# Issuing the last 64 rows of a projection weight before its first 384 rows, at the head of a transfer-bound decode kernel

## The chip, the cores and the metric

The kernel runs on one core of one Trainium2 chip. The metric is device time in microseconds (us) of one execution; a kernel's time is the median of its runs. "The trace" is one profiled execution. In a trace, PE is the matmul engine, DVE the vector engine, ACT the scalar engine, POOL the general one, and SP the engine whose sequencer issues nearly all transfers here; "SPq" is that sequencer. PEld stands for PE's weight loads. A transfer is moved in packets (here of up to 64 KB) by 16 transfer engines. It is issued when SP hands it over, and it has landed when its last bytes have arrived. L438 is line 438 of the kernel.

## The reference, cut to what matters

One token attends to a cache of 65536 positions (16 query heads, 8 key/value heads, head size 256). A small gated block is added. All data are bfloat16.

```
q      = x @ wq                           # x: [1,448]   wq: [448,4096]
scores = einsum(q, k_cache) / 16          # k_cache: [8, 65536, 256]
p      = softmax(scores)
a      = einsum(p, v_cache) @ wo          # v_cache: [8, 65536, 256], wo: [4096,448]
h      = relu(x @ W_gate) * (x @ W_up)    # [448,1792] each
b      = h @ W_down
g      = sigmoid(sum(x * gate_w))
out    = g * a + (1 - g) * b
```

The two caches are 512 MiB. Everything else is some 12 MB.

## The kernel before: the parts that matter here

A planner collects operations with a key, sorts each engine's operations by key, and adds the semaphore waits. A transfer's key is thus its place in SP's order. A cache tile of 8 MB is 128 partitions of 64 KB; three such buffers form a ring. The projection weights at the start borrow the third buffer.

wq has 448 = 3 x 128 + 64 rows. The first 384 are loaded as three rows per partition (24 KB contiguous, "the long rows"), the last 64 as half a row per partition (4 KB, "the short rows"). The matmuls of q need both.

```
for kind, i, t in issue:
    if kind == "wq":
        l_["wq"]  = dma("sp", t,        "wq",  ... dma_start(wq3, A_wq[0:NR3, :].rearrange("(p k) n -> p (k n)", k=R3)))
        l_["wqh"] = dma("sp", t + 0.01, "wqh", ... dma_start(wqh, A_wq[NR3:D, :].rearrange("r (t n) -> (r t) n", t=2)))
        l_["q"]   = mop("pe", tq, f_q, [l_["wq"], l_["wqh"], q0])
        ...                                # q is spread into xm, which the scores need
    elif kind == "gu":                     # gate and up weights: long and short rows each
        ...
    elif kind == "wd":                     # lands over wq, so it waits for q
        a3 = dma("sp", t, "wd", ..., [l_["q"]])
    elif kind == "k":
        kd = dma("sp", t, "r%d" % sl, ... dma_start(ring[sl][:], k_src(n)), free(("k", n)))
```

SP's order at the start is: wq long, wq short, first k tile, gate and up weights, then (after q is computed) wd, then k tiles and v tiles as buffers come free.

## Time and profile before

The time before is 1277.79 us (median of 3 runs, 1277.51 to 1278.08).

| what | value | view |
|---|---|---|
| bytes moved, mean rate | 549.22 MB, 430 GB/s | transfers of the page |
| share of the span in which PE, DVE, ACT are busy | 33%, 50%, 5% | busy times of the page |
| long rows of wq: issue, then time to landing | 0.72 us, 10.5 us | timeline, table of issues |
| short rows of wq: issue, then time to landing | 1.19 us, 11.3 us | timeline, table of issues |
| first q matmul, end of q | 12.53 us, 21.46 us | timeline |
| first DVE work on the k tile | 31.82 us | timeline |

From the page of the kernel before: busy times, then the span in 40 slices with the busy tenths of the transfer engines and the rate in each slice, then packet counts.

```profile
PE 426.9 (33%) x4568; PEld 167.3 (13%) x4568; DVE 633.4 (50%) x421; ACT 63.3 (5%) x124; POOL 4.1 (0%) x21
...
DMA  9999999999999999999999999999999999999998
GB/s 398 443 433 430 435 429 438 435 431 429 435 433 440 428 429 435 433 440 429 431 435 431 438 431 433 435 431 432 438 431 431 435 431 438 433 429 435 415 444 348
DMA packets 12948, 549.22 MB, mean 430 GB/s; under 512 B 1283, under 2 KB 3590, under 8 KB 3974
```

The transfers are 90% or more busy in every slice but the last, at an even rate. No compute engine comes near that. The time is the bytes divided by the rate, plus a short head and a short tail.

Table of transfer issues of the kernel before: destination and source, engine, count, KB each, us from issue to landing.

```profile
ring<-in_A_wq_dram SPq DMA_DIRECT2D x1, 3072.0 KB, 10.5
...
ring<-in_A_wq_dram SPq DMA_DIRECT2D x1, 512.0 KB, 11.3
ring<-in_A_k_cache_dram SPq DMA_DIRECT2D x32, 51.3
ring<-in_A_v_cache_dram SPq DMA_DIRECT2D x31, 33.5
```

A tile takes about 19.4 us to move, but 33 to 51 us (medians) from issue to landing: the queue behind the 16 engines is never empty in the steady state.

Timeline of the kernel before, the lines that matter of its first 35 us: start, length, engine, line, operation, and in brackets how long the engine was idle before it and what ended that.

```profile
0.72 0.40 SPq L437 DMA_DIRECT2D ring<-in_A_wq_dram  x1
1.19 0.41 SPq L438 DMA_DIRECT2D ring<-in_A_wq_dram  x1
1.65 0.43 SPq L483 DMA_DIRECT2D ring<-in_A_k_cache_dram  x1
...
12.53 8.93 PE L341 MATMUL QN<-ring,P_sb 128*128 128x512 bf16 x32 [3.12 <-DMA ring<-in_A_wq_dram]
...
21.49 0.33 SPq L471 DMA_DIRECT2D ring<-in_B_W_down_dram  x1
...
31.82 4.50 DVE L367 STREAM_TRANSPOSE ring<-ring 128x2048 uint32<-128x2048 uint32 x2 [7.50 <-DMA ring<-in_A_k_cache_dram]
```

SP issues the next transfer (wd, L471) as soon as q ends at 21.49 us. At that time the queue still holds the k tile and the gate and up weights, so q is early.

### The profile page before, as it was taken

Reading aid. Unit: us, or ns where it says so; the run is one execution under the profiler, and the core shown is the slowest. Engines: PE = TensorE matmul, PEld = TensorE weight load, DVE = VectorE, ACT = ScalarE, POOL = GpSimd, SP = SyncE. Lnnn points to the kernel's source line nnn. Section 1 sums busy time; section 2 is a strip of 40 time slices with the busy share of each in tenths; the row PEclk is TensorE's granted clock in tenths of the full one; section 3 lists DMA queues with packets and bytes.
Section 4 is the critical chain, followed back from the end, with each engine's and each line's share of the span. In section 5 each row is a group of like instructions: output and inputs, shape, how many; then the busy total and the mean of one; then the engine's idle time right before and its main releaser. Section 6 shows DMA issues by size and latency. Waiting matters only on the chain. (4 is left out here: it accounts for less than half of the span.)

```text
span 1276.2 us, 10216 instructions
## 1 busy us (share of the span) xinstructions
PE 426.9 (33%) x4568; PEld 167.3 (13%) x4568; DVE 633.4 (50%) x421; ACT 63.3 (5%) x124; POOL 4.1 (0%) x21
## 2 busy tenths in 40 slices
PE   3633322334223431224331343321333313233255
PEld 1501110111001210002110111100111101011021
DVE  2698633465433655434555444555434655335600
ACT  0000000010000100001000010000100001000000
POOL 1000000000000000000000000000000000000000
PEclk9656666656666565666656666656666656666565
DMA  9999999999999999999999999999999999999998
GB/s 398 443 433 430 435 429 438 435 431 429 435 433 440 428 429 435 433 440 429 431 435 431 438 431 433 435 431 432 438 431 431 435 431 438 433 429 435 415 444 348
DMA packets 12948, 549.22 MB, mean 430 GB/s; under 512 B 1283, under 2 KB 3590, under 8 KB 3974
## 3 DMA queue, kind: packets, MB, share of 16 engines
q1 hardware_dynamic: 12930, 549.03, 99.7%
q8 instruction: 8, 0.13, 0.0%
q14 instruction: 6, 0.05, 0.0%
q10 hardware_dynamic: 4, 0.00, 0.0%
HBM read 549.03 MB, written 0.00 MB: 430 GB/s over the span
## 5 line engine op out<-in xcount | busy, mean ns | idle before, releaser
L367 DVE STREAM_TRANSPOSE ring<-ring 128x2048 uint32<-128x2048 uint32 x256 | 565.4, 2275 | 396.5 <-DMA ring<-in_A_k_cache_dram 396.5
L378 PE MATMUL ST<-ring,xc 128*16 128x512 bf16 x2048 | 223.9, 611 | 745.6 <-PEq L86 745.6
L378 PEld LDWEIGHTS ST<-ring,xc 128*16 128x16 bf16 x2048 | 68.3, 120 | 887.0 <-issue 886.1
L409 PE MATMUL O<-ring,ptp 128*4 128x512 bf16 x2048 | 150.7, 457 | 32.7 <-DMA ring<-in_A_v_cache_dram 18.7
L494 ACT ACTIVATE P_sb<-ST,nmb 128x512 bf16<-128x512 f32 x32 | 45.1, 1410 | 1102.2 <-DVE nmb L492 1102.2
L492 DVE TENSOR_REDUCE nmb<-ST 128x1 f32<-128x512 f32 x32 | 22.0, 689 | 116.8 <-PE ST L378 116.8
L409 PEld LDWEIGHTS O<-ring,ptp 128*4 128x4 bf16 x2048 | 56.4, 99 | 126.6 <-issue 69.3
L419 DVE CAST o_sb<-O 128x512 bf16<-128x512 f32 x8 | 5.5, 691 | 78.6 <-PE O L409 78.6
L513 DVE TENSOR_TENSOR P_sb<-P_sb,hs 128x1024 bf16<-128x1024 bf16 x16 | 18.9, 1221 | 9.4 <-ACT hs L507 9.4
L518 PE MATMUL PT<-identb,P_sb 128*128 128x128 bf16 x128 | 16.2, 307 | 16.8 <-PEq L86 15.8
L459 PE MATMUL M_ps<-xT,ring 128*128 128x1 bf16 x84 | 9.5, 205 | 17.2 <-DMA ring<-in_B_W_up_dram 17.2
L518 PEld LDWEIGHTS PT<-identb,P_sb 128*128 128x128 bf16 x128 | 12.4, 138 | 19.2 <-issue 19.2
L527 ACT COPY ptp<-PT 128x256 bf16<-128x256 bf16 x32 | 10.3, 375 | 23.9 <-PE PT L518 23.9
L341 PE MATMUL QN<-ring,P_sb 128*128 128x512 bf16 x32 | 8.9, 448 | 3.1 <-DMA ring<-in_A_wq_dram 3.1
L459 PEld LDWEIGHTS M_ps<-xT,ring 128*128 128x128 bf16 x84 | 7.2, 152 | 17.8 <-issue 17.4
L494 ACT ACTIVATION_READ_ACCUMULATOR P_sb<-ST,nmb 128x1 f32 x32 | 8.4, 262 | 0.0
L462 PE MATMUL M_ps<-xT,ring 128*64 128x1 bf16 x56 | 7.8, 276 | 0.0
L442 DVE STREAM_TRANSPOSE scr<-P_sb 128x256 uint32<-128x256 uint32 x1 | 0.4, 445 | 12.5 <-ACT P_sb L441 12.5
L503 PE MATMUL M_ps<-identf,hs 128*2 128x128 f32 x8 | 2.5, 308 | 11.1 <-PEq L86 11.1
L539 DVE RECIPROCAL hs<-M_ps 128x2 f32<-128x2 f32 x8 | 1.4, 170 | 8.3 <-PE M_ps L538 8.3
L462 PEld LDWEIGHTS M_ps<-xT,ring 128*64 128x64 bf16 x56 | 5.4, 191 | 0.4
L389 PE MATMUL A_ps<-ring,attnT 128*1 128x224 bf16 x64 | 4.6, 306 | 0.7 <-DMA ring<-in_A_wo_dram 0.6
(74 smaller groups left out, 65.7 us busy)
## 6 DMA issues: line engine op xcount, KB each, us to landing
ring<-in_A_v_cache_dram SPq DMA_DIRECT2D x1, 4096.0 KB, 23.6
ring<-in_A_wq_dram SPq DMA_DIRECT2D x1, 3072.0 KB, 10.5
ring<-in_A_wo_dram SPq DMA_DIRECT2D x1, 2240.0 KB, 38.3
ring<-in_A_v_cache_dram SPq DMA_DIRECT2D x1, 2048.0 KB, 28.2
ring<-in_B_W_down_dram SPq DMA_DIRECT2D x1, 1568.0 KB, 21.7
ring<-in_B_W_gate_dram SPq DMA_DIRECT2D x1, 1344.0 KB, 32.9
ring<-in_B_W_up_dram SPq DMA_DIRECT2D x1, 1344.0 KB, 35.5
ring<-in_A_v_cache_dram SPq DMA_DIRECT2D x1, 1024.0 KB, 30.2
```

The lines of the kernel that those rows point to most:

```text
L341: ins = e.matmul(QN_ps, xw3[:, k_, 31 - h:159 - h], rhs, start=(h == 0 and kt == 0), stop=(h == H - 1 and kt == R3))
L367: return lambda e: e.transpose(v, v)
L378: ins = e.matmul(bank[32 * w:32 * w + 16, :], xc[:, x0:x0 + 16], ktv[sl][:, u0:u0 + 16, c, :, r_], start=(b == 0 and c == 0 and r_ == 0), ...
L409: ins = e.matmul(OP[32 * g:32 * g + 4, :], ptp[:, col:col + 13:4], ring[sl][:, k * 512:(k + 1) * 512], start=(a == 0 and k < 4), stop=(a = ...
L419: o1 = op("dv", tn, lambda e: e.tensor_copy(o_sb[:], OP[:]), [pv[n], last.get(("otr", h - 1))])
L459: e.matmul(GU_ps[:, c:c + 1], wf3[which][:, kt * F + ft:(kt + 1) * F:FT], xT[:, kt:kt + 1], start=(kt == 0), stop=False, skip_group_check= ...
L462: ins = e.matmul(GU_ps[64 * half:64 * half + 64, c:c + 1], wfh[which][:, ft:F // 2:FT], xT[:, R3 + half:R3 + half + 1], start=False, stop= ...
L492: smax[n] = op("dv", tk + 22, lambda e, n=n, NM=NM, t_=t_: e.tensor_reduce(NM[:, t_:t_ + 1], ST[n % 2][:], AX.X, ALU.max, negate=True), [q ...
L494: aexp[n] = op("ac", tk + 23, lambda e, n=n, t_=t_, NM=NM, RS=RS: e.activation(P_sb[:, t_:2048:4], ST[n % 2][:], ACTF.Exp, bias=NM[:, t_:t ...
L513: rsc = op("dv", tt, lambda e, X=X, pb=pb: e.tensor_tensor(pb, pb, X[:, 12:16].unsqueeze(1).to_broadcast([128, 256, 4]), ALU.mult), [h7, a ...
L518: ins = e.transpose(PT[rd][:, s * 128:(s + 1) * 128], P_sb[:, (rd * 8 + s) * 128:(rd * 8 + s + 1) * 128], identb[:, :])
L527: ins = e.copy(dst, src)
```

## The change

The intent: the short rows are small and were the last thing that q waited for, so they go first.

```diff
-                l_["wqh"] = dma("sp", t + 0.01, "wqh", lambda e: e.dma_start(wqh, A_wq[NR3:D, :].rearrange("r (t n) -> (r t) n", t=2)))
+                l_["wqh"] = dma("sp", t - 0.01, "wqh", lambda e: e.dma_start(wqh, A_wq[NR3:D, :].rearrange("r (t n) -> (r t) n", t=2)))
```

No bytes, packets or instructions change; two issues on SP swap places.

## The prediction

> **What bounds the kernel now.** The transfers. The page of the profile gives 549.22 MB in a span of 1276.2 us, a mean of 430 GB/s, and the DMA row of its slices is 9 (90% or more busy) in 39 of 40 slices, at 428 to 443 GB/s in all but the first (398) and the last few. The Trainium skill ("DMA: Bandwidth & Descriptors", section "Where 436 GB/s comes from") puts the ceiling of the 16 SBUF ports at 435 GB/s; this trace's slices lie at it. DVE is 50% busy, PE 33%. The chain of waits holds the end of the transfers (32.48 us of wo), then about 3 us of PE and DVE work.
>
> **What the change does.** No bytes, packets or instructions are added or removed. The order of instructions shows one difference on the SP queue: the 512 KB transfer of wq's last 64 rows (128 x 2048, 4 KB per partition) is issued before the 3072 KB one (128 x 12288, 24 KB per partition).
>
> **Costing it.**
> - Issue: the timeline shows the two issues at 0.72 and 1.19 us, 0.40 and 0.41 us long, the k tile's at 1.65. Swapped, k stays at about 1.65.
> - A gap behind the small transfer? At 430 GB/s its 512 KB are an estimated 1.2 us of work, and the next issue follows 0.47 us after it, so the engines should not run dry.
> - The first consumer, the q projection on PE (line 341), waits for both transfers. The table of issues gives 10.5 us to landing for the long one (0.72 + 10.5 = 11.2 us) and 11.3 us for the short (1.19 + 11.3 = 12.5); PE starts at 12.53. After the change the short one should land early (an estimated 3 to 5 us) and the long one at about 12.5, since the same 3.5 MB lie ahead.
> - If q shifts, it has room: it ends at 21.49 us and releases only the issue of wd, while the queue already holds the k tile and the gate and up weights, which land until about 39.5 us. That is 18 us of slack. Later tiles are issued with 33 to 51 us to landing, so the queue never empties.
>
> **On the critical path:** essentially nothing. Only the start could move: when the first bytes flow, and the skew of the 16 engines. The one microsecond from 1 to 2 us shows 271 GB/s, so a change of at most some 0.3 us there is thinkable in either direction.
>
> **Predicted time:** 1277.7 us; 8 times in 10 between 1276.0 and 1279.6 us (run to run 0.6 us before). Faster by over 2%: 0.5%; within 2%: 99%; slower by over 2%: 0.5%.
>
> **What would show it right:** the same 549.22 MB, 12948 packets and 430 GB/s; DMA slices all 9; SP issues short, then long, then k at about 1.65 us; the short transfer landing within about 5 us of its issue and the long one taking about 11.5 us; PE's first q matmul at 12.0 to 13.0 us; k's first transpose on DVE at about 31.8 us as before.
> **Wrong:** a first slice well under or over 398 GB/s, a hole in the DMA windows between 1 and 4 us, or a k tile landing a microsecond or more earlier or later.
>
> **What would make it wrong:** small 4 KB packets first starting the engines unevenly, with a skew that lasts to the end; or a cost of the first transfer that depends on its size.

## The result

The changed kernel takes 1277.46 us (median of 6 runs, 1277.28 to 1277.77) against 1277.65 us (median of 6, 1277.39 to 1278.08). The ratio is 0.9998 with a 95% interval of 0.9986 to 1.0011: the same. Ratios here are the mean time of one kernel's fast runs over that of the other's of the same rounds, so not quite the ratio of the medians quoted.

From the page of the changed kernel, the same lines.

```profile
DMA  9999999999999999999999999999999999999998
GB/s 401 448 427 428 436 431 440 433 429 431 436 438 436 428 429 438 436 436 429 429 438 431 438 433 429 433 436 434 436 431 429 436 433 436 433 431 436 405 446 354
DMA packets 12948, 549.22 MB, mean 430 GB/s; under 512 B 1283, under 2 KB 3590, under 8 KB 3974
```

Table of transfer issues of the changed kernel.

```profile
ring<-in_A_wq_dram SPq DMA_DIRECT2D x1, 3072.0 KB, 10.4
...
ring<-in_A_wq_dram SPq DMA_DIRECT2D x1, 512.0 KB, 3.4
```

Timeline of the changed kernel.

```profile
0.73 0.40 SPq L438 DMA_DIRECT2D ring<-in_A_wq_dram  x1
1.19 0.41 SPq L437 DMA_DIRECT2D ring<-in_A_wq_dram  x1
1.65 0.43 SPq L483 DMA_DIRECT2D ring<-in_A_k_cache_dram  x1
...
11.67 8.87 PE L341 MATMUL QN<-ring,P_sb 128*128 128x512 bf16 x32 [3.81 <-DMA ring<-in_A_wq_dram]
...
20.58 0.33 SPq L471 DMA_DIRECT2D ring<-in_B_W_down_dram  x1
...
31.01 4.50 DVE L367 STREAM_TRANSPOSE ring<-ring 128x2048 uint32<-128x2048 uint32 x2 [7.60 <-DMA ring<-in_A_k_cache_dram]
```

The start did change. q begins 0.86 us earlier, wd is issued 0.91 us earlier, and the k tile is usable 0.81 us earlier. The span moved from 1276.2 to 1276.1 us. So two questions are left: where did 0.8 us go, and was it the change's at all?

**Where it went.** The Trainium skill ("DMA: Bandwidth & Descriptors", section "Why a DMA increments its semaphore by 16 and not by 1") says that a transfer runs on up to 16 engines which finish independently, and that only the full count of 16 means that the data have landed. The trace agrees: it has 16 completions for each large transfer, 0.4 to 4 us apart in the six traces of the two kernels. From these records I worked out the first, mean and last completion, in us from the start of the span:

```
                       k tile 0             tile before 868 us       next tile                last transfer of all
                       first mean  last     first  mean   last       first  mean   last       first   mean    last
before                 30.73 31.00 31.80    854.89 855.99 857.59     874.25 875.41 877.25     1272.08 1272.77 1273.92
before, 2nd look       30.73 31.03 31.64    854.91 856.00 857.04     874.26 875.41 877.30     1272.63 1273.06 1274.13
before, 3rd look       30.84 31.47 33.28    854.99 856.42 858.98     874.35 875.83 878.33     1273.42 1274.00 1275.14
after                  30.54 30.73 30.99    854.84 855.77 856.85     874.19 875.18 877.10     1272.25 1272.77 1273.86
after, 2nd look        30.49 30.76 30.98    854.80 855.76 856.88     874.14 875.18 877.20     1272.42 1272.90 1274.06
after, 3rd look        30.43 30.66 30.96    854.73 855.65 856.72     874.08 875.06 876.97     1271.71 1272.48 1273.69
```

A consumer waits for the last of the 16, and the last is what came 0.81 us earlier at the k tile. The mean, which counts the work of all engines, came only 0.27 us earlier. The two leads were lost at different places.

*The lead of the last engine.* While the queue does not run dry, an engine that is late can stay late: in the first two profiles (before and after) the last completion is still 0.74 us apart at 857 us. It need not: in the second look of before the last completion there, 857.04, is only 0.16 us behind the second look of after. Between the first two profiles the lead is then lost in one tile. The latest five of the 16, in nanoseconds after the tile's first:

```
           tile before 868 us              next tile
before     1623 1667 2020 2051 2693        1621 1676 2040 2709 3003
after      1621 1725 1788 1918 2010        1633 1738 1789 2001 2908
```

In both kernels one engine drops by some 0.9 to 1 us in this tile and becomes the last (the records do not name the engines; this is read from the sorted times): in before it was among those at 2020 and 2051 (the old last, 2693, is still there at 2709), in after it was at 1918 or 2010. The last engine of the start is no longer the last engine, and so its lead is worth nothing any more: 877.25 against 877.10 us. Both traces hold an 8 KB instruction packet of 0.33 us at 868.5 and 868.4 us, which may be what this engine was kept by; that is inferred from the time alone, no run takes the packet away.

*The lead of the mean.* It is untouched by this: 0.22 to 0.24 us in the first and second looks, at 857 us and still at 1210 us. Most of it goes in the next tile (0.02 and 0.09 us are left), where the queue nearly runs dry. SP can issue that tile only when PE is done with the scores of the last k tile (releaser PE ST L378 in SP's waits), and these wait for DVE's transposes, which wait for the last of the k tile's 16 completions. Timelines of before and then of after, window 1185 to 1209 us, the lines of this chain:

```profile
1186.91 17.66 DVE L367 STREAM_TRANSPOSE ring<-ring 128x2048 uint32<-128x2048 uint32 x8 [12.18 <-DMA ring<-in_A_k_cache_dram]
1204.77 3.29 PE L378 MATMUL ST<-ring,xc 128*16 128x512 bf16 x32 [5.16 <-PEq L86]
1208.11 0.34 SPq L550 DMA_DIRECT2D ring<-in_A_v_cache_dram  x1
```

```profile
1186.78 17.66 DVE L367 STREAM_TRANSPOSE ring<-ring 128x2048 uint32<-128x2048 uint32 x8 [12.59 <-DMA ring<-in_A_k_cache_dram]
1204.63 3.59 PE L378 MATMUL ST<-ring,xc 128*16 128x512 bf16 x32 [5.15 <-PEq L86]
1208.27 0.34 SPq L550 DMA_DIRECT2D ring<-in_A_v_cache_dram  x1
```

At the issue only one transfer of 2240 KB is left in the queue, and the first engine is done with it about 1 us later (in the third look of before, 0.2 us earlier). From the completions and the packets, in us ("engines idle" is the mean over the 16 engines from 1205 to 1232 us; most other tiles follow each other at 19.35):

```
                    DVE starts     issue of    mean completion           from mean   engines
                    on k tile      next tile   2240 KB      next tile    to mean     idle
before              1186.91        1208.11     1210.36      1230.03      19.67       0.07
before, 2nd look    1186.97        1208.43     1210.34      1230.18      19.84       0.13
before, 3rd look    1188.00        1209.49     1210.72      1231.22      20.50       0.71
after               1186.78        1208.27     1210.13      1230.01      19.88       0.20
after, 2nd look     1186.94        1208.43     1210.12      1230.09      19.97       0.29
after, 3rd look     1186.68        1207.88     1210.00      1229.72      19.72       0.15
```

From here on the transfers follow this issue: over all 14 traces of this document the next tile's mean completion comes 21.7 to 22.1 us after it. In the first pair the changed kernel's k tile was usable 0.13 us earlier, but its last matmuls took 0.30 us longer (3.59 against 3.29), so the issue came 0.16 us later and the engines that were ahead stood idle. At the end the means are equal and the last completions 0.06 us apart. The third look of after had the early issue and kept its 0.3 us. This is read from the traces; no run changes this wait.

### The profile page after: what moved, and what is told of

Its sections match the earlier page's. It is cut to its first block, busy times and chain, and to the rows that moved or that the text cites. A ratio compares the mean times of both kernels' runs of the same rounds, so it can differ in the third digit from the quotient of the medians.

```text
span 1276.1 us, 10216 instructions
## 1 busy us (share of the span) xinstructions
PE 427.3 (33%) x4568; PEld 167.5 (13%) x4568; DVE 633.2 (50%) x421; ACT 63.3 (5%) x124; POOL 4.6 (0%) x21
## 2 busy tenths in 40 slices
DMA packets 12948, 549.22 MB, mean 430 GB/s; under 512 B 1283, under 2 KB 3590, under 8 KB 3974
## 5 line engine op out<-in xcount | busy, mean ns | idle before, releaser
L378 PE MATMUL ST<-ring,xc 128*16 128x512 bf16 x2048 | 222.8, 608 | 745.5 <-PEq L86 745.5
L378 PEld LDWEIGHTS ST<-ring,xc 128*16 128x16 bf16 x2048 | 68.0, 120 | 886.1 <-issue 884.8
L492 DVE TENSOR_REDUCE nmb<-ST 128x1 f32<-128x512 f32 x32 | 22.1, 689 | 116.8 <-PE ST L378 116.8
```

The source lines that it names most:

```text
L378: ins = e.matmul(bank[32 * w:32 * w + 16, :], xc[:, x0:x0 + 16], ktv[sl][:, u0:u0 + 16, c, :, r_], start=(b == 0 and c == 0 and r_ == 0), ...
L492: smax[n] = op("dv", tk + 22, lambda e, n=n, NM=NM, t_=t_: e.tensor_reduce(NM[:, t_:t_ + 1], ST[n % 2][:], AX.X, ALU.max, negate=True), [q ...
```

## The experiments

Theory A: the total of the transfers is the time; q's start has slack; only an empty queue would cost. Rival B: the start of q lies on the critical path, and its gain is kept or should be.

### The changed kernel and the kernel before, again

No edit. First the changed kernel in five rounds:

> The changed kernel once more, in five rounds. Theory A (the transfers' total is the time; the start of q has slack): ratio 0.9999 to 1.0000 of before, at most 0.3 us shorter. Rival B (what q gains at the start is kept to the end): about 0.8 us shorter, ratio 0.9994. In its profile, if the earlier q start belongs to the change and not to one execution: short rows landed about 3.4 us after issue, first q matmul near 11.7 us, k tile's first transpose near 31.0 us.

Measured: 1277.55 us (5 runs, 1277.37 to 1277.64) against 1277.88 us (9 runs, 1277.35 to 1278.06), ratio 0.9998, interval 0.9984 to 1.0011, just outside what theory A was given. First q matmul at 11.63 us, k tile at 31.00 us.

> The kernel before against itself: ratio 1.0000; how far it is off says what a difference of a few tenths of a microsecond is worth. In its profile, if the late q start belongs to the order: first q matmul near 12.5 us, k tile's first transpose near 31.8 us. If it was one execution's: between 11.6 and 12.6 us.

Measured: 1277.59 us (1277.47 to 1277.86) against the same 1277.88 us, ratio 0.9999, interval 0.9985 to 1.0013. First q matmul at 12.37 us, k tile at 31.67 us.

> One more look at the changed kernel, for the spread of the start from execution to execution: first q matmul 11.5 to 11.9 us if the earlier start belongs to the change.

Measured: first q matmul at 11.66 us, k tile at 30.98 us. (The state of a single run is unknown; single runs serve here for positions in the trace, not for times.)

> One more look at the kernel before: first q matmul 12.3 to 12.7 us if the late start belongs to the order; nearer 11.7 us if it was one execution's.

Measured: first q matmul at 12.37 us; the run was 1278.65 us, and being single its state is unknown.

What follows: the earlier q start belongs to the change (11.63 to 11.67 us in three traces, 12.37 to 12.53 us in three of before). Against the same 9 runs the changed kernel was 0.33 us shorter and the kernel before itself 0.29 us shorter. So a few tenths of a microsecond can't be told apart here, but the 0.8 us of rival B is not there. A weaker rival is left open: over all runs the medians are 1277.70 us for before (36 runs, single ones included) and 1277.46 for after (12), so some 0.2 us of the mean's lead may on average be kept.

The odd run before_look is instructive, with the caution that it is one run. Some of its engines were held up between 12 and 33 us: the last completion of the k tile came at 33.28 us, 1.49 us later than in the first trace of before. The last completion of the last transfer came 1.22 us later, at 1275.14, and the span was 1.2 us longer, 1277.4. The table above shows how: at 1210 us the mean was only some 0.4 us behind that of the first trace of before, but the last engine's lag delayed the last k tile by 1.09 us and the issue behind it by 1.38, the other engines stood idle, and the mean was 1.19 us behind at 1231. A lag of the last engine costs the span where a wait for it lets the queue run dry.

### Moving q by much more than the change does

First the gate and up weights in front of wq:

```diff
-  a1.append(dma("sp", t + 0.01 * i_, "wf%d" % i_, ...
+  a1.append(dma("sp", 2.5 + 0.01 * i_, "wf%d" % i_, ...
-  a1.append(dma("sp", t + 0.01 * i_ + 0.005, "wfh%d" % i_, ...
+  a1.append(dma("sp", 2.5 + 0.01 * i_ + 0.005, "wfh%d" % i_, ...
```

(In this and the following cuts "..." stands for the rest of a line, which is unchanged.)

> The gate and up weights (3136 KB) go in front of wq, so q starts an estimated 7.3 us later (3.21 MB at 430 GB/s), near 19.8 us and ends near 28.8 us. Theory A (q has some 18 us of slack before the queue would empty): same time, within 0.5 us of before. Rival B (the start of q is on the critical path): 7 us longer, about 1285 us.

Timeline of this kernel.

```profile
19.67 9.59 PE L341 MATMUL QN<-ring,P_sb 128*128 128x512 bf16 x32 [11.00 <-DMA ring<-in_A_wq_dram]
29.29 0.33 SPq L471 DMA_DIRECT2D ring<-in_B_W_down_dram  x1
```

Measured: 1278.38 us (4 runs, 1277.67 to 1278.53) against 1277.66 us, ratio 1.0006, interval 0.9989 to 1.0023; the profiled run's span was 1276.3 us. q came 7.1 us later and the time moved by 0.7 us in the median, a little more than the half microsecond expected, and by 0.1 us in the profiled span. Rival B, with 7 us, falls. Whether the 0.7 us is real stays open.

Then the first k tile in front of wq:

```diff
-  kd = dma("sp", t, "r%d" % sl, ...
+  kd = dma("sp", t if n else 2.0, "r%d" % sl, ...
```

> The first k tile (8192 KB) goes in front of wq: q starts near 32 us and ends near 41 us, some 1.5 us after the queue has emptied (about 39.4 us). Theory A: the engines stand idle for an estimated 2.5 us (with about 1 us from issue to first bytes), and the time grows by 2 to 3.5 us, to about 1280 us. Rival B: 19.5 us longer, about 1297 us. A theory that nothing of the order matters: no change.

And both edits together:

> The k tile and the gate and up weights go in front of wq, so that wq lands last of all that is queued, near 39.4 us; q takes 9 us or more, and only its end lets the next transfer be issued. Theory A: a hole of some 10 us in the DMA windows after 39 us and a time 9 to 13 us longer, about 1288 us; behind the hole the 16 engines start level again. Rival B (the start of q sets the time): 27 us longer.

Measured: k_first 1283.36 us (1282.62 to 1285.13), ratio 1.0047, interval 1.003 to 1.0063. kgu_first 1291.83 us (1290.92 to 1292.62), ratio 1.0113, interval 1.0096 to 1.013; before was 1277.66 us.

Busy times by stretch: the stretch, its length, the busy time (instruction count) of the five engines, the share of its full clock that PE was granted, the transfers' busy share and rate (GB/s). First before, then k_first, then kgu_first.

```profile
38.00:42.00 4.00, 2.30 (x25) 2.19 (x25) 4.00 (x3) 0.00 (x0) 0.00 (x0) 0.50 1.33 560
65.00:70.00 5.00, 0.00 (x0) 0.00 (x0) 5.00 (x4) 0.00 (x0) 0.00 (x0) 0.50 1.05 449
```

```profile
38.00:42.00 4.00, 3.17 (x15) 1.19 (x13) 0.44 (x1) 0.59 (x1) 0.00 (x0) 1.00 0.17 40
65.00:70.00 5.00, 4.36 (x58) 2.63 (x50) 0.59 (x1) 0.00 (x0) 0.00 (x0) 0.79 1.06 359
```

```profile
38.00:42.00 4.00, 2.95 (x8) 1.03 (x9) 0.00 (x0) 0.00 (x0) 0.00 (x0) 1.00 0.03 10
42.00:50.00 8.00, 6.76 (x27) 2.67 (x25) 0.82 (x4) 0.59 (x1) 0.00 (x0) 1.00 0.10 17
```

(A packet's bytes are counted in the stretch in which it starts, so a short stretch can show more than the engines can move.) In k_first the transfers stand at 40 GB/s from 38 to 42 us, in kgu_first at 10 and 17 GB/s from 38 to 50 us: the queue has run dry, because wd can only be issued after q. This is theory A's cost of an empty queue, and the only way in which q's start was seen to reach the time. It came where the slack had been used up.

The size was underestimated: 5.7 us against 2 to 3.5, and 14.2 against 9 to 13. The completions show why. In k_first, wd's mean landing is 4.4 us later than before and the next k tile's 4.3 us; the tile after that is 6.1 us later, and all later ones stay at 6.0 to 6.1. So there are two holes. The first is longer than expected since I had let the queue last until 39.4 us, which is when the slowest engine's data landed; the others were done at about 38.5 us. The second is at 65 us: the third buffer is freed by the projection over wd, which is late too. SP's waits, before and then k_first (line, releaser, total us, times, longest):

```profile
SPq L471 <- PE QN L341: 17.2, 1, 17.2
SPq L483 <- PE A_ps L389: 34.2, 1, 34.2
```

```profile
SPq L471 <- PE QN L341: 36.6, 1, 36.6
SPq L483 <- PE A_ps L389: 22.8, 1, 22.8
```

In k_first SP is released from this second wait at 64.52 us, 0.9 us before the packets of the tile before run out; the first packets of 64 KB after that take 2.5 to 3.5 us, where before they take 2.42.

kgu_first also shows that its engines did not start level again, as I had expected: behind the hole wd's completions are 1.33 us apart and the next tile's 2.71 us.

### What makes the earlier start: which small transfer goes first

These runs ask why the last completion of wq came earlier at all. First the short rows of the gate weights (224 KB, 1.8 KB per partition) in front, wq as before:

```diff
-  a1.append(dma("sp", t + 0.01 * i_ + 0.005, "wfh%d" % i_, ...
+  a1.append(dma("sp", t + 0.015 if i_ else 2.0, "wfh%d" % i_, ...
```

> wq stays long before short, but the 224 KB of the gate's short rows (1.8 KB per partition) go first of all. If small packets in front start the 16 engines more evenly, whichever tensor they belong to: the 16 completions of wq within 0.6 us of each other (1.09 before, 0.49 after the change), and q starts near 12.4 us although 0.53 us more lies ahead of it. If the short rows of wq are what matters: spread near 1.1 us and q near 13.0 us. The time is the same as before within 0.5 us either way.

Then the first 4 KB per partition of the long rows as a transfer of their own (q waits for all three):

```diff
-  l_["wq"] = dma("sp", t, "wq", ... dma_start(wq3, src))
+  l_["wq0"] = dma("sp", t - 0.01, "wq0", ... dma_start(wq3[:, 0:2048], src[:, 0:2048]))
+  l_["wq"]  = dma("sp", t,        "wq",  ... dma_start(wq3[:, 2048:], src[:, 2048:]))
```

> The order of before (long rows, then short ones), but the first 4 KB of each partition's long rows are a transfer of their own, the first of all; 20 KB and the short rows follow. If it is the 24 KB packets at the very start that start the 16 engines late and unevenly: as after the change, the last wq completion falls some 0.8 us earlier than before (q starts at 11.5 to 11.9 us, not 12.4) and the mean landing of the k tile is 0.2 to 0.35 us earlier (30.65 to 30.8 us instead of 31.0). If the gain at the start came of the short rows not standing alone behind the long ones: q at 12.3 to 12.6 us as before. The time stays within 0.5 us of before either way.

> The kernel of long_split once more, for one look: if its missing gain belongs to the kernel, the k tile's mean landing is 31.0 to 31.2 us and q starts at 12.4 to 12.7 us again; if it was one execution's, 30.65 to 30.8 us and 11.6 to 11.9 us.

Then the first 4 KB per partition of the k tile in front:

```diff
+  k0 = None if n else dma("sp", 2.0, "k0", ... dma_start(ring[sl][:, 0:2048], k_src(n)[:, 0:2048]))
+  # and the rest of tile 0 in its old place; its transposes wait for both
```

> wq stays long before short, but the first 4 KB per partition of the k tile (512 KB) go in front of it as a transfer of their own. If small packets of any tensor in front do it: q starts near 12.9 us (12.5 plus 1.2 us for the 512 KB, less 0.8 us), the k tile's mean landing 0.2 to 0.35 us earlier than before. If only the short rows of wq do it: q near 13.7 us, the k tile at 31.0 us. The time stays within 0.5 us of before either way.

Last the order slice of the long rows, short rows, rest of the long rows (the cut is against long_split):

```diff
-  l_["wq"]  = dma("sp", t,        "wq", ... dma_start(wq3[:, 2048:], src[:, 2048:]))
+  l_["wq"]  = dma("sp", t + 0.02, "wq", ... dma_start(wq3[:, 2048:], src[:, 2048:]))
```

> The 4 KB slices of the long rows first, then the short rows, then the other 20 KB of the long rows: 8 KB per partition in small packets before the first large one. If it is enough of small packets in front that makes the gain (1 MB here), q starts at 11.5 to 11.9 us and the k tile's mean landing is 30.65 to 30.8 us. If slices at a pitch of 24 KB are themselves slow, whatever follows, q starts near 12.5 us and the k tile lands at 31.0 us or later.

Measured, with the bytes that the packet records give for the first 5 us:

| kernel | goes first | q starts, us | k tile lands, mean, us | moved by 5 us, KB | time, us (runs) |
|---|---|---|---|---|---|
| before (3 traces) | wq long, 24 KB rows | 12.37 to 12.53 | 31.00, 31.03, 31.47 | 944 to 973 | 1277.65 (6) |
| after (3 traces) | wq short, 4 KB | 11.63 to 11.67 | 30.66 to 30.76 | 1097 to 1110 | 1277.46 (6) |
| kpart_first | 4 KB slices of k | 12.86 | 30.65 | 1133 | 1277.47 (4) |
| gs_first | 1.8 KB rows of gate | 12.79 | 31.54 | 991 | 1277.46 (4) |
| long_split | 4 KB slices of wq long | 12.60 | 31.13 | 954 | 1277.92 (4) |
| long_split_look | the same | 12.64 | 31.23 | 894 | 1277.91 (1) |
| slice_short_rest | slices, then short rows | 12.88 | 31.50 | 784 | 1277.88 (1) |

In gs_first 224 KB more lie ahead of q and of the k tile, an estimated 0.53 us at 430 GB/s, so its q start is worth 12.26 us and its k tile 31.01 us: next to no gain over before, and wq's 16 completions are still 1.04 us apart. In kpart_first 512 KB more lie ahead of q, an estimated 1.2 us; its q start is worth 11.66 us, as in after, and its k tile lands as early as in after. So the early start is not bound to the short rows of wq. Neither do small packets alone bring it: the slices of the long rows are 4 KB packets too, and with them nothing was gained, or something lost.

Where it comes from in the records: the first 16 packets of 24 KB take 1.63 to 1.76 us on average in the three traces of before, and 0.96 to 1.05 us in those of after, behind the short rows; the usual time is 0.91 us. In after the start-up is spent on the short rows' packets, and by 5 us some 0.12 to 0.17 MB more have moved, an estimated 0.3 to 0.4 us at 430 GB/s. That is the gain of the mean completion. Why 4 KB slices of the long rows (24 KB apart) don't do the same as the short rows (without gaps) or slices of k (256 KB apart) was not settled.

All of these are within 0.3 us of before. The medians lean the way of the start (1277.46 and 1277.47 where it is early, about 1277.9 where it is late), but gs_first, without an early start, is at 1277.46 too, and no interval leaves 1 out.

## Why the prediction was right, point by point

- **What bounds the kernel: right.** The changed kernel has the same 549.22 MB, 12948 packets and 430 GB/s. The Trainium skill ("DMA: Bandwidth & Descriptors", section "Where 436 GB/s comes from") gives 435 GB/s as the ceiling of the ports; the mean of both traces, 430, agrees with it. (Single slices reach 448, but a packet's bytes are counted where it starts.)
- **No gap behind the small transfer: right.** The k tile is still issued at 1.65 us, and more had moved by 5 us than before, not less.
- **The short rows land early: right.** 3.4 us after issue.
- **The step that failed: "the long one at about 12.5, since the same 3.5 MB lie ahead", and with it q at 12.0 to 13.0 us and the k tile "at about 31.8 us as before".** q started at 11.67 us and the k tile was usable at 31.01 us. Equal bytes give an equal mean, and the mean indeed moved only 0.3 us: the later of the two wq transfers completed at 11.65 us in before and at 11.34 in after. But a consumer waits for the last of 16 engines, and with large packets first that one was 0.8 us behind the mean (12.44), in after 0.3 us (11.63).
- **"A change of at most some 0.3 us there is thinkable": right for the mean of the engines** (0.27 us at the k tile), too small for the last one (0.81 us).
- **Slack of some 18 us behind q: right, and shown.** 7.1 us later cost 0.7 us in the median, which the interval does not tell from nothing; some 19 us later, with q ending at 40.9 us, emptied the queue and cost 5.7 us.
- **"So the queue never empties": wrong in one place.** At 1208 us a tile is issued with about 1 us of work left for the first engine, and engines stood idle for 0.07 us in before and 0.20 in after. There the changed kernel's lead of the mean went, 0.23 us in the first pair, of which 0.02 was left.
- **The time: 1277.7 predicted, 1277.46 measured.** The transfers' total decides it, as predicted. The skew that the prediction named as its risk was there, but with small packets first it was smaller, not larger. That the first pair ends so close is in part luck: the third look of after, 0.36 us ahead at 1210 us, kept 0.3 us to its end.

## What to carry to other kernels

Where one queue keeps the transfer engines full from start to end, reordering the first loads moves when consumers start but not when the last byte lands; ask instead which wait could let the queue run dry, since here that alone was shown to cost time (5.7 and 14.2 us). Look for it near the end too: the slices of the page show 9 tenths where the completions show a queue that nearly ran dry. Read a landing as the last of 16 engines: an earlier landing can be a smaller spread and no more throughput, and then its gain can end when another engine becomes the last. Before believing some tenths of a microsecond, time the old kernel against itself; here that gave 0.29 us.

## What the Trainium skill lacked or had wrong

- "DMA: Bandwidth & Descriptors", section "Where 436 GB/s comes from", says that for transfers from HBM the HBM side, about 358 GB/s for a core, binds. This case read 549 MB from HBM at 430 GB/s over the whole span. The sentence is too general rather than the page wrong throughout: its measured table has 425 GB/s for one large transfer with the other core idle, and keeps 358 for two cores that both stream.
- The same page says nothing of the packets just after a start or an empty queue: here the first 16 packets of 24 KB took 1.63 to 1.76 us on average against 0.91 us later, and behind the short second hole of k_first packets of 64 KB took 2.5 to 3.5 us against 2.42.
- The same page says that the 16 engines finish independently, but not how long a lag can stay while the queue holds work: 16 completions of one transfer were up to 4 us apart, a start-up lag of the last engine was still there after 800 us in one pair of traces (0.74 us) and mostly gone in another (0.16), and one of 1.49 us lengthened a span by 1.2 us once a wait for the last engine held back the next issue.
